# ScalarE's queue between the products, an uneven split of the second matmul, and an interleaved change of layers in a fused attention and two-layer kernel

## The chip, the cores and the metric

The kernel runs on one core of a Trainium2 chip. The metric is the device time of one execution in microseconds (us). The engines are named as in the profile: PE is TensorE (PEld its weight loads), DVE is VectorE, ACT is ScalarE, POOL is GpSimd, SP is SyncE, which here issues the DMAs.

## The reference

```
attn: q, k, v (8 batches, 8 heads, 576 tokens, 64 wide), in chunks of 64 tokens
      softmax(q_c k_c^T / 8) v_c                     -> x, 4608 tokens x 512
layer 1: h = x @ w_in (512 x 2048); g = s * relu(h)**2 + b; y = g @ w_out (2048 x 512)
layer 2: h = y @ w2_in;  P = a0 + a1 h + a2 h^2 + a3 h^3
         Q = 1 + |b0||h| + |b1| h^2;  g = P / (Q + 1e-6);  out = g @ w2_out
```

Everything is float32; the moe weights arrive as 64-bit floats, which the kernel decodes on DVE.

## The kernel before

**Blocks.** The 4608 tokens are 36 tiles of 128 in ten blocks. Blocks 0 and 1 (two tiles each) go through layer 1 in float32, while the weights are loaded and decoded. Blocks 2 to 9 (four tiles each) use fp16 pairs, a high and a low part of each number, and three matmuls for a product of two pairs. Attention of later tiles, decoding of layer 2's weights, and the scaling of finished blocks run beside the matmuls of earlier blocks.

**A group.** The first matmul of layer 1 is done by one level of a Strassen scheme: seven products of 12 matmuls of 256 columns (`product`, L445). `l1_group(j, u, ...)` computes a quarter (u = 0 to 3) of block j's 2048 hidden columns, so there are 32 groups. A group has four quarters. (0) Products 1 and 7 go into two PSUM banks, Z and Y; ACT copies Y to SBUF (L504) and then Z over Y (L505). (1) Products 2 and 6 follow, 2 into Y and 6 into Z; ACT takes Y out with a relu (L512) and copies Z over Y again (L513). (2) Products 4 and 5; DVE adds the earlier copy to each and thereby empties both banks (L518, L519); ACT does relu, square and the fp16 rounding (L521, L491, L492), DVE the low part (L493). (3) Product 3 into Z, and the same for the other half (L526, L491, L492, L493). The next group's Z and Y use the same two banks, so its product 7 needs the bank that L526 empties.

**What fills the gaps.** After each of the four quarters stands a piece of the *second* matmul of the group before: `m2(n)` issues the 12 matmuls of 512 columns of quarter `QO[n]` (L484). So PE has other work while ACT makes the copy that product 2 or product 4 waits for. Four PSUM banks collect y; when a block is complete, ACT takes them out (L547).

**Jobs.** `at(slot, fn, ...)` puts other work into slots, four slots to a group, and `jobs_at(n)` runs those of a slot at the head of a quarter: attention (`at_amx` squares v on ACT, L232, once v is loaded; `at_score` L263; `at_exp` L274 to L276; `at_prob` L287 to L290; `at_pv` L311, whose result goes from PSUM to the block's x by an ACT copy, L315), the splitting of x and y into fp16 pairs by pieces (`x_piece`, `y_piece`: L414 on ACT, L415 on DVE, seven for a block in the order `YORD`), and the decoding of layer 2's weights on DVE (L141 to L144, L586) after a DMA has brought them (L130). There is one x tile for the block being assembled: the next block's first L315 has to wait until all seven pieces of the block before have been read. The score of a tile goes into two PSUM banks, one of which the attention's second product uses as well.

**The order.** Instructions are written in one program order, and a scheduler decides, engine by engine, in which order they are queued, from the dependencies and a model of durations. Each engine then runs its queue in that order. `tc.issue_after(ins)` adds an edge: what is traced under it is queued behind `ins` on the engine of `ins`.

**Layer 2** does the same with the second set of weights and a longer chain on ACT and DVE (`chain_a` to `chain_e`, L946 to L978). Its second matmul lags two groups behind, so its first two groups have none of it between their products. The change of layers: the last group's second matmul (48 matmuls) and the last twelve before it stand in one run, then layer 2's group 0 begins; its copies on ACT are L1049, L1061, L937 and L1071.

Of the kernel before, what the change touches and what calls it, by code (L numbers as in the profile page):

```python
# [20 lines left out]
def attn_moe_moe2(ctx: ExitStack, tc: tile.TileContext, qk, v, w_in, w_out, s_in, b_in,  # L21
# [28 lines left out]
    wo1_p = ctx.enter_context(tc.tile_pool(name="wo1", bufs=KF + 1, reuse_waits="tile"))  # L50
    wi1a_p = ctx.enter_context(tc.tile_pool(name="wi1a", bufs=14, reuse_waits="tile"))
    y1_p = ctx.enter_context(tc.tile_pool(name="y1", bufs=1, reuse_waits="tile"))
    ps_y = ctx.enter_context(tc.tile_pool(name="psy", bufs=1, space=PS))
# [338 lines left out]

    YORD = ("11", "T3", "21", "T1", "22", "T2", "T4")
    t2 = {}
# [77 lines left out]

    gq = {}

    def l1_y2(j, u, q):
        if u + q == 2 and u == 0:
# [4 lines left out]
        for dd in range(KD):  # L481
            for m, (a, l) in enumerate(TERMS):
                o = a * 512 + dd * 128
                T.matmul(out=ybank[j][dd], lhsT=wo1.hl[f][:, o:o + 128], rhs=g[:, l],  # L484
                         start=(first and m == 0), stop=(last and m == 2))
        if q == 1:
            gq.pop((j, u))
# [7 lines left out]
    def l1_group(j, u, jobs_at, m2):  # L495
        x = xhl[j]
        bank = lambda nm: ps_h.tile([128, 2, 256], F32, name=nm, tag="h")
        half = lambda: l1_p.tile([128, 2, 2, 256], F32, name="h1", tag="h1")
        jobs_at(0)
        Z, Y = bank("bZ"), bank("bY")  # L500
        product(wi1, x, u, "1", Z, True)
        product(wi1, x, u, "7", Y, True)
        p7 = l1_p.tile([128, 2, 256], F32, name="sn", tag="sn", bufs=3)
        A.activation(out=p7, in_=Y, func=AF.Copy)  # L504
        A.activation(out=Y, in_=Z, func=AF.Copy)  # L505
        m2(0)
# [4 lines left out]
        g = gq[j, u] = l1_p.tile([128, 2, 2, 1024], F16, name="g", tag="g")  # L511
# [143 lines left out]
    def l2_consts():  # L655
# [19 lines left out]
        V.tensor_tensor(out=dlt, in0=dlt, in1=bt[:, 0:1], op=ALU.mult)  # L675

    start = [KF * j for j in range(NB + 1)]
# [37 lines left out]
    bufs = ((y1_p, "y32"), (raw_p, "raw"), (l1_p, "g"), (l1_p, "g"))  # L715

# [33 lines left out]

    at(start[3], l2_consts)

    if True:
# [75 lines left out]
        g_step()  # L829
        while pend_y:  # L830
            y_step()

        prev = None
        QO = (2, 3, 0, 1)

        def m2_of(u):
            def m2(n):
                if u is None:
                    return
                l1_y2(*u, QO[n])  # L840
                if u[1] == 3 and n == 3:
                    y_later(u[0])
            return m2
# [3 lines left out]

        def l1_slot(slot):
            j, k = slot // KF, slot % KF
            run_jobs(slot)  # L850
            if j == NB - 1:
# [10 lines left out]
        for j in range(NFULL, NB):  # L862
            if j == NB - 1:
                right.close()
                w2_p = ctx.enter_context(tc.tile_pool(name="w2", bufs=14, side="right", reuse_waits="tile"))
                w2_fetch(quads[0])
            for u in range(4):
                l1_group(j, u, lambda n: l1_slot(start[j] + 4 * u + n), m2_of(prev))
                prev = (j, u)
        m2 = m2_of(prev)  # L870
        for n in range(4):
            m2(n)
        while wo2.todo:
            wo2.fetch(wo2.todo.pop(0))
        while wo2.cut:
            wo2.split(wo2.cut.pop(0))
        late = sorted(jobs)
        left.close()
# [3 lines left out]
        yin = {}  # L882
        par = {}
# [8 lines left out]
        def l2_par(j):  # L892
            tn = lambda n, nm: l2_p.tile([128, n], F32, name=nm, tag=nm, bufs=3)
            c = tn(1, "c")
            V.scalar_tensor_tensor(out=c, in0=invy[j], scalar=16.0, in1=wi2.inv, op0=ALU.mult, op1=ALU.mult)
            m = tn(4, "m")
            hb = tn(1, "hb")
            V.tensor_scalar(out=hb, in0=c, scalar1=2.0 ** 26 * float(DM) ** 0.5, scalar2=None, op0=ALU.mult)
            V.memset(m[:, 0:1], 1.0)
            V.tensor_tensor(out=m[:, 1:2], in0=hb, in1=rb[:, 0:1], op=ALU.min)  # L900
            V.tensor_tensor(out=m[:, 2:3], in0=hb, in1=hb, op=ALU.mult)
            V.tensor_tensor(out=m[:, 2:3], in0=m[:, 2:3], in1=rb[:, 1:2], op=ALU.min)
            V.tensor_tensor(out=m[:, 3:4], in0=m[:, 2:3], in1=hb, op=ALU.mult)
            V.tensor_tensor(out=m, in0=m, in1=aabs, op=ALU.mult)
            gm = tn(1, "gm")
            V.tensor_reduce(out=gm, in_=m, axis=AX.X, op=ALU.add)
            V.tensor_scalar(out=gm, in0=gm, scalar1=TINY, scalar2=None, op0=ALU.max)
            e = l2_p.tile([128, 1], I32, name="ge", tag="ge", bufs=3)
            V.tensor_scalar(out=e, in0=gm.bitcast(I32), scalar1=EXPMASK, scalar2=None, op0=ALU.bitwise_and)
            ig = tn(1, "ig")  # L910
            V.tensor_scalar(out=ig, in0=e.bitcast(F32), scalar1=2.0 ** -14, scalar2=None, op0=ALU.mult)
            na = tn(4, "na")
            V.reciprocal(out=na[:, 0:1], in_=ig)
            for i in range(1, 4):
                V.tensor_tensor(out=na[:, i:i + 1], in0=na[:, i - 1:i], in1=c, op=ALU.mult)
            V.tensor_tensor(out=na, in0=na, in1=a2_sb, op=ALU.mult)
            bc = tn(1, "bc")
            V.tensor_tensor(out=bc, in0=gam, in1=c, op=ALU.mult)
            ao = tn(1, "ao")
            V.tensor_tensor(out=ao, in0=ig, in1=wo2.inv, op=ALU.mult)  # L920
            par[j] = (na, bc, ao)

# [41 lines left out]
        def chain_d(i, sl):  # L964
            na, bc, ao = par[seq[i][0]]
            if sl[0] == 0:
                s2[i].append(l2_p.tile([128, 2, BIG], F16, name="g2", tag="g2", bufs=2))
            v, e, r = (t[:, sl[0]:sl[1]] for t in s2[i][:3])
# [32 lines left out]
        l2_load(0)  # L1001
        l2_par(0)
        prime = ps_a.tile([128, 512], F32, name="prime", tag="x")
# [4 lines left out]
        for i in range(N):  # L1008
            for q in range(4):
# [5 lines left out]
                m4[step][slot].append((i, q))  # L1015
        late = [fn for slot in late for fn in jobs.pop(slot)]
        extra = {}
        for n, (fn, args) in enumerate(late):
            if fn is y_piece:
                extra.setdefault(4 + 2 * YORD.index(args[1]), []).append((fn, args))  # L1020
            else:
                extra.setdefault(2, []).append((fn, args))

        def run_m4(i, slot):
            for u in m4[i][slot]:
                l2_y(*u)

        for i in range(N + 2):
            cur, c = i < N, i - 1
            sl = (parts if c in (0, N - 1) else full) if 0 <= c < N else []  # L1030
            if cur:
                j, u = seq[i]
                if u == 1 and j + 1 < NB2:
                    l2_par(j + 1)
# [76 lines left out]
```

## Time and profile before

| | |
|---|---|
| runs | 1607.34, 1609.14, 1614.02 us (median 1609.14) |
| profiled execution | 1607.84 us, of which the profile's span is 1606.0 |
| busy share of the span | PE 96%, DVE 82%, ACT 60% |
| mean granted TensorE clock | 0.988 |
| layer 1 in fp16 | about 160 to 871 us |
| change of layers | about 871 to 907 us |
| layer 2 | about 907 to 1606 us |

A share of busy time is a mean over the whole span; what a stage waits for has to be read from that stage. Times in the trace are counted from the start of the span, and the 1.8 us outside it are in the run's time alone.

### The profile page before, as it was taken

What the parts mean: (1) busy time and instruction counts of PE and PEld (TensorE: products, weight loads), DVE (VectorE), ACT (ScalarE), POOL (GpSimd) and SP (SyncE); (2) the same over time, 40 slices, a digit from 0 to 9 for tenths busy, and PEclk for the clock granted to TensorE, in tenths of its full rate; (3) what the DMA queues carried; (4) which work ended last, traced back from release to release, by engine and by line L of the source; (5) the groups of instructions that cost most, each with busy time, mean ns of one, the idle gap of its engine ahead of it and who ended that gap; (6) DMA issues with size and microseconds to landing.
All of it is one profiled execution on the core that took longest, in us unless ns stands there. A gap on an engine that the chain in (4) does not pass through costs nothing.

```text
span 1606.0 us, 29660 instructions
## 1 busy us (share of the span) xinstructions
PE 1540.4 (96%) x12501; PEld 1042.7 (65%) x12501; DVE 1315.2 (82%) x1980; ACT 966.9 (60%) x1268; POOL 21.9 (1%) x57
## 2 busy tenths in 40 slices
PE   7999999899998999999999899999999999999998
PEld 6878666566665656666665666666666666666664
DVE  7998768778787777665683999999998989888887
ACT  3577856555664655656675756555555565656564
POOL 0000000000000000000000000000000000000000
PEclk8999999999999999999999999999999999999999
DMA  7722214435343353311133020101010101010100
GB/s 278 272 86 62 59 48 163 159 99 171 106 139 128 119 165 96 99 30 57 41 125 115 24 73 27 47 27 47 27 47 27 47 28 47 27 47 28 33 27 27
DMA packets 86118, 131.43 MB, mean 82 GB/s; under 512 B 39648, under 2 KB 39648, under 8 KB 85984
## 3 DMA queue, kind: packets, MB, share of 16 engines
q1 hardware_dynamic: 85984, 129.53, 24.9%
q8 instruction: 98, 1.61, 0.4%
q14 instruction: 36, 0.29, 0.1%
HBM read 86.77 MB, written 34.34 MB: 75 GB/s over the span
## 4 chain that ended last, share of the span: by engine, by line
PE 54%; DVE 26%; ACT 10%; DMA 5%; issue 5%; POOL 0%; SPq 0%; POOLq 0%; ACTq 0%; DVEq 0%
PE y L989 21%; PE bZ L445 13%; PE bY L445 8%; PE y L484 6%; PE bC L445 2%; DVE bits L143 2%; DVE wf L144 2%; ACT h L491 2%; DVE yhl L415 2%; DMA raw<-in_moe_w_in_dram 1%; ACT g L492 1%; DMA raw<-in_moe_w_out_dram 1%; ACT h L521 1%; DVE bits L141 1%; DVE whl L620 1%
## 5 line engine op out<-in xcount | busy, mean ns | idle before, releaser
L445 PEld LDWEIGHTS <-whl 128*128 128x128 f16 x5712 | 560.2, 99 | 164.7 <-issue 50.8
L445 PE MATMUL bZ<-xhl,whl 128*128 128x256 f16 x3264 | 406.2, 275 | 2.8 <-ACT sn L937 1.1
L989 PE MATMUL y<-whl,g 128*128 128x512 f16 x1728 | 396.1, 379 | 3.1 <-DVE g L978 3.1
L484 PE MATMUL y<-g,whl 128*128 128x512 f16 x1536 | 352.3, 379 | 1.0 <-ACT y L547 0.8
L445 PE MATMUL bY<-xhl,whl 128*128 128x256 f16 x2016 | 252.1, 276 | 37.3 <-ACT bY L505 20.2
L989 PEld LDWEIGHTS <-g 128*128 128x128 f16 x1728 | 168.7, 98 | 178.7 <-DVE g L978 4.6
L484 PEld LDWEIGHTS <-whl 128*128 128x128 f16 x1536 | 150.3, 98 | 156.6 <-issue 2.1
L1071 ACT ACTIVATE h<-bZ 128x512 f32<-128x512 f32 x36 | 21.4, 595 | 235.6 <-PE bZ L445 188.4
L493 DVE TENSOR_TENSOR g<-h,g 128x1024 f16<-128x1024 f32 x64 | 78.3, 1223 | 75.9 <-ACT g L492 75.8
L955 DVE SCALAR_TENSOR_TENSOR v<-v,c 128x2048 f32<-128x2048 f32 (+1 forms) x42 | 85.7, 2044 | 37.3 <-ACT v L946 37.3
L956 DVE TENSOR_TENSOR e<-e,h 128x2048 f32<-128x2048 f32 (+1 forms) x42 | 83.0, 1981 | 10.1 <-ACT e L947 10.1
L970 DVE SCALAR_TENSOR_TENSOR g<-e,na,r 128x2048 f16<-128x2048 f32 (+1 forms) x42 | 85.7, 2045 | 5.5 <-ACT r L962 2.4
L957 DVE SCALAR_TENSOR_TENSOR e<-e,na,h 128x2048 f32<-128x2048 f32 (+1 forms) x42 | 85.7, 2045 | 0.8
L977 DVE SCALAR_TENSOR_TENSOR e<-e,na,v 128x2048 f32<-128x2048 f32 (+1 forms) x42 | 85.7, 2044 | 0.8
L971 DVE SCALAR_TENSOR_TENSOR v<-v,g 128x2048 f32<-128x2048 f32 (+1 forms) x42 | 83.2, 1984 | 1.0
L978 DVE TENSOR_TENSOR g<-e,r 128x2048 f16<-128x2048 f32 (+1 forms) x42 | 82.9, 1977 | 0.1
L947 ACT ACTIVATE e<-h,na 128x2048 f32<-128x2048 f32 (+1 forms) x42 | 77.2, 1842 | 6.8 <-DVE g L978 6.8
L946 ACT ACTIVATE v<-h,bc 128x2048 f32<-128x2048 f32 (+1 forms) x42 | 73.6, 1756 | 7.7 <-DVE h L1065 6.5
L961 ACT ACTIVATE r<-v,c 128x2048 f32<-128x2048 f32 (+1 forms) x42 | 73.5, 1755 | 1.0 <-DVE v L955 1.0
L962 ACT ACTIVATE r<-r,c 128x2048 f32<-128x2048 f32 (+1 forms) x42 | 73.3, 1755 | 1.0
L491 ACT ACTIVATE h<-h 128x1024 f32<-128x1024 f32 x64 | 67.5, 1054 | 1.6
L492 ACT ACTIVATE g<-h 128x1024 f16<-128x1024 f32 x64 | 67.5, 1054 | 1.6
(189 smaller groups left out, 1767.8 us busy)
## 6 DMA issues: line engine op xcount, KB each, us to landing
qk<-in_qk_dram SPq DMA_DIRECT2D x36, 512.0 KB, 3.5
raw<-in_moe_w_in_dram SPq DMA_DIRECT2D x16, 1024.0 KB, 5.5
raw<-in_moe_w_out_dram SPq DMA_DIRECT2D x16, 1024.0 KB, 5.8
v<-in_v_dram SPq DMA_DIRECT2D x36, 256.0 KB, 2.7
out_dram<-o SPq DMA_DIRECT2D x36, 256.0 KB, 2.1
yd<-yhl SPq DMA_DIRECT2D x27, 256.0 KB, 2.2
xhl<-yd SPq DMA_DIRECT2D x27, 256.0 KB, 2.6
w2din<-wf SPq DMA_DIRECT2D x16, 256.0 KB, 2.0
```

The costliest lines, as they stand in the source:

```text
L445: T.matmul(out=b[:, s, :], lhsT=t[:, a, o:o + 128], rhs=x[pk][:, l, kk, :], start=start and s + kk + n == 0, stop=stop and s + kk + n == 4 ...
L484: T.matmul(out=ybank[j][dd], lhsT=wo1.hl[f][:, o:o + 128], rhs=g[:, l], start=(first and m == 0), stop=(last and m == 2))
L491: A.activation(out=hf, in_=hf, func=AF.Square)
L492: A.activation(out=g[:, 0], in_=hf, func=AF.Copy)
L955: V.scalar_tensor_tensor(out=v, in0=v, scalar=dlt, in1=v, op0=ALU.add, op1=ALU.mult)
L956: V.tensor_tensor(out=e, in0=e, in1=hh, op=ALU.mult)
L957: V.scalar_tensor_tensor(out=e, in0=e, scalar=na[:, 1:2], in1=hh, op0=ALU.add, op1=ALU.mult)
L970: V.scalar_tensor_tensor(out=g[:, 0], in0=e, scalar=na[:, 0:1], in1=r, op0=ALU.add, op1=ALU.mult)
L971: V.scalar_tensor_tensor(out=v, in0=v, scalar=q0c, in1=g[:, 0], op0=ALU.add, op1=ALU.mult)
L977: V.scalar_tensor_tensor(out=e, in0=e, scalar=na[:, 0:1], in1=v, op0=ALU.add, op1=ALU.subtract)
L978: V.tensor_tensor(out=g[:, 1], in0=e, in1=r, op=ALU.mult)
L989: T.matmul(out=ybank[j][t], lhsT=g[:, a, q, t * 128:(t + 1) * 128], rhs=w[:, l * 512:(l + 1) * 512], start=(u + q == 0 and m == 0), stop=( ...
```

## The change

1. In a group, `jobs_at(n, ins)` passes an ACT instruction, and the slot's jobs are traced under `issue_after` of it: in quarter 0 the last group's relu of product 3, in quarter 1 the first copy of Z over Y, in quarters 2 and 3 the second one.
2. The sixteen parts of the second matmul (four quarters q by four output banks dd, three matmuls each) are dealt to the four gaps as 5, 5, 4, 2 instead of 4, 4, 4, 4. The remaining steps of the float32 second matmul go into the gaps of the first group.
3. `YORD` puts piece 22 last; the x pieces lie in slots 0, 0, 1, 2, 2, 3, 4 counted from the first instead of 0, 0, 1, 1, 2, 2, 3.
4. The last group's second matmul goes between the products of layer 2's group 0. The splits of layer 2's output weights that were left over follow at the ends of its groups 0 and 1, and `l2_par` of blocks 0 and 1 (some twenty DVE instructions on a few columns each) moves into layer 1's last block. The g tiles of both layers share one pool.

```diff
-    YORD = ("11", "T3", "21", "T1", "22", "T2", "T4")
+    YORD = ("11", "T3", "21", "T1", "T2", "T4", "22")
...
-        jobs_at(0)
+        jobs_at(0, crit.get("h"))
...
-        A.activation(out=Y, in_=Z, func=AF.Copy)
+        c = A.activation(out=Y, in_=Z, func=AF.Copy)
         m2(0)
-        jobs_at(1)
+        jobs_at(1, c)
...
-        A.activation(out=Y, in_=Z, func=AF.Copy)
+        c = A.activation(out=Y, in_=Z, func=AF.Copy)
         m2(1)
-        jobs_at(2)
+        jobs_at(2, c)
...
-        jobs_at(3)
+        jobs_at(3, c)
         product(wi1, x, u, "3", Z, False, True)
-        A.activation(out=h0[:, :, 1], in_=Z, func=AF.Relu, scale=16.0 * C1)
+        crit["h"] = A.activation(out=h0[:, :, 1], in_=Z, func=AF.Relu, scale=16.0 * C1)
...
+    XS = (0, 0, 1, 2, 2, 3, 4)
...
-            at(slot + 1 + m // 2, x_piece, j, p)
+            at(slot + 1 + XS[m], x_piece, j, p)
...
-        while pend_y:
-            y_step()
...
-        QO = (2, 3, 0, 1)
+        M2U = [(q, dd) for q in (2, 3, 0, 1) for dd in range(KD)]
+        M2C = (0, 5, 10, 14, 16)
...
                 if u is None:
+                    if pend_y:
+                        y_step()
                     return
-                l1_y2(*u, QO[n])
+                for q, dd in M2U[M2C[n]:M2C[n + 1]]:
+                    l1_y2(*u, q, dd)
...
-            run_jobs(slot)
+            with tc.issue_after(after.ins) if after else ExitStack():
+                run_jobs(slot)
...
-        m2 = m2_of(prev)
-        for n in range(4):
-            m2(n)
...
+        last_m2 = m2_of(prev)
...
+            if i == 0:
+                last_m2(slot)
```

ACT's queue before, in the last group of block 3 (the stretch from about 318 us). `wsq` is the squared v, `xhl` a piece of x, `sn` and `bY<-bZ` the two copies, `h<-bY` the relu, `e` the exponential of the attention:

```order
L232 ACTIVATE wsq,am<-v 128x512
L414 ACTIVATE xhl<-x_3144,c_238 128x512
L414 ACTIVATE xhl<-tx,c_238 128x512
L414 ACTIVATE xhl<-x_3144,c_238 128x512
L504 ACTIVATE sn<-bY 128x512
L414 ACTIVATE xhl<-x_3144,c_238 128x512
L505 ACTIVATE bY<-bZ 128x512
L512 ACTIVATE h_4318<-bY 128x2x256
L414 ACTIVATE xhl<-x_3144,c_238 128x512
L276 ACTIVATE e<-e 128x512
L513 ACTIVATE bY<-bZ 128x512
```

The same group in the changed kernel (lines are one higher, L506 and L514 are the copies of Z over Y):

```order
L505 ACTIVATE sn<-bY 128x512
L506 ACTIVATE bY<-bZ 128x512
L290 ACTIVATE ph<-e 128x512
L415 ACTIVATE xhl<-x_3149,c_241 128x512
L415 ACTIVATE xhl<-tx,c_241 128x512
L513 ACTIVATE h_4324<-bY 128x2x256
L514 ACTIVATE bY<-bZ 128x512
L277 ACTIVATE e<-e 128x512
L415 ACTIVATE xhl<-x_3149,c_241 128x512
L233 ACTIVATE wsq,am<-v 128x512
L415 ACTIVATE xhl<-x_3149,c_241 128x512
```

The square of v, the pieces of x and the exponential have moved from in front of the two copies to behind them.

ACT's queue in the changed kernel behind that group, in the first group of block 4 (`x_3149` is the x of the block before, `x_4400` the next block's, written by L316 from the bank `xp`):

```order
L505 ACTIVATE sn<-bY 128x512
L506 ACTIVATE bY<-bZ 128x512
L290 ACTIVATE ph<-e 128x512
L415 ACTIVATE xhl<-x_3149,c_241 128x512
L316 ACTIVATE x_4400<-xp,xsc 128x4x128
L513 ACTIVATE h_4622<-bY 128x2x256
L514 ACTIVATE bY<-bZ 128x512
```

The last piece of the old x now stands behind this group's copies, and the first L316 of the new x behind that piece; before, the L315 that answers to it stood in the group before, ahead of that group's relu L526.

The same first group of block 4 further on, before, from the relu of products 4 and 5 to that of product 3 (L491 and L492 are square and rounding, `vs` is v scaled for the attention, `y` the output banks):

```order
L521 ACTIVATE h_4617<-h_4617 128x1024
L491 ACTIVATE h_4617<-h_4617 128x1024
L492 ACTIVATE g<-h_4617 128x1024
L315 ACTIVATE x_4395<-xp,xsc 128x4x128
L246 ACTIVATE vs<-v,sc 128x512
L526 ACTIVATE h_4616<-bZ 128x2x256
```

And in the changed kernel:

```order
L522 ACTIVATE h_4623<-h_4623 128x1024
L492 ACTIVATE h_4623<-h_4623 128x1024
L548 ACTIVATE y_4778<-y_3623,c_257,al 128x512
L493 ACTIVATE g<-h_4623 128x1024
L316 ACTIVATE x_4400<-xp,xsc 128x4x128
L548 ACTIVATE y_4778<-y_3624,c_257,al 128x512
L527 ACTIVATE h_4622<-bZ 128x2x256
```

The scaling L246 has gone behind the relu of product 3, and two of the four evictions of y have come ahead of it. This is so in the first groups of seven blocks; in most other groups the scaling alone has left, and in one of four L315 with it.

At the change of layers, in ACT's queue between layer 2's copies L1071 (now L1078) and L1049 (now L1056), two of the four parts of `chain_a` (L946, L947) have moved ahead of the first, and two evictions of layer 1's last y and one more split of an output weight (L184, now L185) have come in.

## Rows read from the trace of the kernel before

**Rows 1.** The page's first part: busy us, share of the span, instructions.

```profile
PE 1540.4 (96%) x12501; PEld 1042.7 (65%) x12501; DVE 1315.2 (82%) x1980; ACT 966.9 (60%) x1268; POOL 21.9 (1%) x57
```

**Rows 2.** Windows: stretch, length, busy us of each engine, clock, DMA.

```profile
160.00:871.00 711.00, 672.19 (x6412) 447.50 (x6410) 517.26 (x1070) 447.35 (x658) 16.16 (x39) 0.99 0.34 107
```

**Rows 3.** PE's waits from 160 to 871 us: total, times, longest.

```profile
PE bY L445 <- ACT bY L505: 20.2, 15, 2.8
PE bY L445 <- ACT bY L513: 14.7, 11, 3.2
PE bY L445 <- ACT h L526: 2.0, 2, 1.2
```

**Rows 4.** Timeline from 280 us: start, length, instruction, idle before and its releaser.

```profile
294.00 0.63 ACT L232 ACTIVATE wsq<-v 128x512 bf16<-128x512 f32 x1 [2.14 <-DMA v<-in_v_dram]
...
295.24 0.58 ACT L505 ACTIVATE bY<-bZ 128x512 f32<-128x512 f32 x1
...
295.88 1.47 PE L445 MATMUL bY<-xhl,whl 128*128 128x256 f16 x12 [1.22 <-ACT bY L505]
...
300.06 0.43 DVE L141 TENSOR_SCALAR bits<-raw 128x512 int32<-128x512 int32 x1 [4.13 <-DMA raw<-in_moe_w_in_dram]
...
303.31 0.63 ACT L276 ACTIVATE e<-e 128x512 f32<-128x512 f32 x1 [5.28 <-DVE e L275]
...
304.48 1.47 PE L445 MATMUL bY<-xhl,whl 128*128 128x256 f16 x12 [3.23 <-ACT bY L513]
...
310.65 1.48 PE L445 MATMUL bZ<-xhl,whl 128*128 128x256 f16 x12
...
313.77 0.71 ACT L246 ACTIVATE vs<-v,sc 128x512 f16<-128x512 f32 x1
...
314.38 0.58 ACT L526 ACTIVATE h<-bZ 128x512 f32<-128x512 f32 x1
...
315.87 1.47 PE L445 MATMUL bY<-xhl,whl 128*128 128x256 f16 x12
...
318.64 0.63 ACT L232 ACTIVATE wsq<-v 128x512 bf16<-128x512 f32 x1 [1.50 <-DMA v<-in_v_dram]
...
322.76 0.58 ACT L505 ACTIVATE bY<-bZ 128x512 f32<-128x512 f32 x1
...
323.39 2.72 PE L445 MATMUL bY<-xhl,whl 128*128 128x256 f16 x12 [2.83 <-ACT bY L505]
```

**Rows 5.** Window behind that last wait; columns as in rows 2.

```profile
323.20:326.70 3.50, 3.31 (x16) 2.31 (x16) 3.47 (x9) 0.64 (x3) 0.00 (x0) 0.51 0.02 8
```

**Rows 6.** Groups by line and shape, 240 to 616 us: count, busy us, mean ns.

```profile
L414 ACT ACTIVATE xhl<-x,c 128x512 f16<-128x512 f32 x20 | 14.2, 712 | 1.8 <-DVE c L391 1.8
...
L415 DVE SCALAR_TENSOR_TENSOR xhl<-x,c,xhl 128x512 f16<-128x512 f32 x19 | 14.2, 746 | 0.1
...
L547 ACT ACTIVATE y<-y,c,al 128x512 f32<-128x512 f32 x16 | 11.4, 769 | 0.0
...
L315 ACT ACTIVATE x<-xp,xsc 128x512 f32<-128x512 f32 x16 | 10.7, 670 | 0.0
...
L289 ACT ACTIVATE ph<-e 128x512 f16<-128x512 f32 x16 | 10.1, 630 | 43.8 <-DVE e L287 43.8
```

**Rows 7.** The chain that ended last: start, time it took, what.

```profile
203.69 2.59 PE y L484 x12
206.28 1.31 PE bY L445 x12
```

**Rows 8.** Timeline of the change of layers; columns as in rows 4.

```profile
891.28 1.47 PE L445 MATMUL bZ<-xhl,whl 128*128 128x256 f16 x12 [1.05 <-ACT sn L937]
...
895.79 0.58 ACT L1071 ACTIVATE h<-bZ 128x512 f32<-128x512 f32 x1
...
902.15 0.58 ACT L1049 ACTIVATE bC<-bZ 128x512 f32<-128x512 f32 x1
...
902.77 0.49 PE L445 MATMUL bC<-xhl,whl 128*128 128x256 f16 x3 [4.12 <-ACT bC L1049]
```

More of the change, by code (lines that the diff above doesn't have):

```diff
@@ L473, in attn_moe_moe2, with l1_y2 @@
     gq = {}
-    def l1_y2(j, u, q):
-        if u + q == 2 and u == 0:
+    crit = {}
+    def l1_y2(j, u, q, dd):
+        if (u, q, dd) == (0, 2, 0):
             ybank[j] = new_y()
@@ L480, in l1_y2 @@
         g = gq[j, u][:, :, q // 2, (q % 2) * 512:(q % 2 + 1) * 512]
[L481 to L486, printed above, removed]
+        for m, (a, l) in enumerate(TERMS):
+            o = a * 512 + dd * 128
+            T.matmul(out=ybank[j][dd], lhsT=wo1.hl[f][:, o:o + 128], rhs=g[:, l],
+                     start=(first and m == 0), stop=(last and m == 2))
+        if (q, dd) == (1, KD - 1):
             gq.pop((j, u))
@@ L675, in l2_consts, with l2_par @@
         V.tensor_tensor(out=dlt, in0=dlt, in1=bt[:, 0:1], op=ALU.mult)
+    par = {}
+    def l2_par(j):
+        tn = lambda n, nm: y1_p.tile([128, n], F32, name=nm, tag="p" + nm, bufs=3 if nm in ("na", "bc", "ao") else 1)
+        c = tn(1, "c")
+        V.scalar_tensor_tensor(out=c, in0=invy[j], scalar=16.0, in1=wi2.inv, op0=ALU.mult, op1=ALU.mult)
+        m = tn(4, "m")
+        hb = tn(1, "hb")
+        V.tensor_scalar(out=hb, in0=c, scalar1=2.0 ** 26 * float(DM) ** 0.5, scalar2=None, op0=ALU.mult)
+        V.memset(m[:, 0:1], 1.0)
+        V.tensor_tensor(out=m[:, 1:2], in0=hb, in1=rb[:, 0:1], op=ALU.min)
+        V.tensor_tensor(out=m[:, 2:3], in0=hb, in1=hb, op=ALU.mult)
+        V.tensor_tensor(out=m[:, 2:3], in0=m[:, 2:3], in1=rb[:, 1:2], op=ALU.min)
+        V.tensor_tensor(out=m[:, 3:4], in0=m[:, 2:3], in1=hb, op=ALU.mult)
+        V.tensor_tensor(out=m, in0=m, in1=aabs, op=ALU.mult)
+        gm = tn(1, "gm")
+        V.tensor_reduce(out=gm, in_=m, axis=AX.X, op=ALU.add)
+        V.tensor_scalar(out=gm, in0=gm, scalar1=TINY, scalar2=None, op0=ALU.max)
+        e = y1_p.tile([128, 1], I32, name="ge", tag="pge", bufs=1)
+        V.tensor_scalar(out=e, in0=gm.bitcast(I32), scalar1=EXPMASK, scalar2=None, op0=ALU.bitwise_and)
+        ig = tn(1, "ig")
+        V.tensor_scalar(out=ig, in0=e.bitcast(F32), scalar1=2.0 ** -14, scalar2=None, op0=ALU.mult)
+        na = tn(4, "na")
+        V.reciprocal(out=na[:, 0:1], in_=ig)
+        for i in range(1, 4):
+            V.tensor_tensor(out=na[:, i:i + 1], in0=na[:, i - 1:i], in1=c, op=ALU.mult)
+        V.tensor_tensor(out=na, in0=na, in1=a2_sb, op=ALU.mult)
+        bc = tn(1, "bc")
+        V.tensor_tensor(out=bc, in0=gam, in1=c, op=ALU.mult)
+        ao = tn(1, "ao")
+        V.tensor_tensor(out=ao, in0=ig, in1=wo2.inv, op=ALU.mult)
+        par[j] = (na, bc, ao)
     start = [KF * j for j in range(NB + 1)]
@@ L751, in attn_moe_moe2 @@
     at(start[3], l2_consts)
+    at(start[NB - 1] + 2, l2_par, 0)
+    at(start[NB - 1] + 3, l2_par, 1)
     if True:
@@ L867, in attn_moe_moe2 @@
             for u in range(4):
-                l1_group(j, u, lambda n: l1_slot(start[j] + 4 * u + n), m2_of(prev))
+                l1_group(j, u, lambda n, c: l1_slot(start[j] + 4 * u + n, c), m2_of(prev))
                 prev = (j, u)
-        m2 = m2_of(prev)
-        for n in range(4):
-            m2(n)
[L873 to L877, printed above, removed]
         left.close()
@@ L890, in l2_load @@
                 yin[j][p] = t
[L892 to L921, printed above, removed]
         seq = [(j, u) for j in range(NB2) for u in range(4)]
@@ L1015, in attn_moe_moe2, with late_jobs @@
                 m4[step][slot].append((i, q))
-        late = [fn for slot in late for fn in jobs.pop(slot)]
         extra = {}
[L1018 to L1022, printed above, removed]
+        def late_jobs():
+            for fn, args in [fn for slot in sorted(jobs) for fn in jobs.pop(slot)]:
+                extra.setdefault(4 + 2 * YORD.index(args[1]) if fn is y_piece else 3, []).append((fn, args))
+            for n in range(len(wo2.cut)):
+                extra.setdefault(n * 2 // len(wo2.cut), []).append((lambda: wo2.split(wo2.cut.pop(0)), ()))
+        last_m2 = m2_of(prev)
         def run_m4(i, slot):
@@ L1026, in run_m4 @@
                 l2_y(*u)
+            if i == 0:
+                last_m2(slot)
+                for _ in range((len(wo2.todo) + 3 - slot) // (4 - slot)):
+                    wo2.fetch(wo2.todo.pop(0))
+                if slot == 3:
+                    late_jobs()
         for i in range(N + 2):
```

13 lines of the change are left out of this document (6 added, 7 removed).

## The prediction

> **What bounds the kernel now.** I read the page's shares first: PE is busy for 96% of the span [rows 1], so what can be won is its idle time and the time that it runs at less than full clock. Then the windows by stage. In the 711 us of layer 1 in fp16, PE is busy for 672.2 [rows 2]; 38.8 us are idle, more than half of the 65.6 of the whole span. Over the same stretch the list of PE's waits has 20.2 us in 15 waits for ACT's copy L505, 14.7 in 11 waits for the copy L513, and 2.0 in two for the relu L526 [rows 3]. Every entry has ACT as the releaser, though ACT is busy for 60% of the span. So it isn't ACT's speed but what stands ahead of the copy in its queue, and the timeline shows it. At 294.00 ACT starts the squaring L232 after 2.14 idle us, released by the DMA that brings v; only behind it run the copies, and product 2 has stood for 1.22 [rows 4]. At 303.31 the exponential L276 starts after 5.28 us of idling; L513 is behind it, and product 4 has waited for 3.23. What the exponential waited for is DVE, which stood for 4.13 us at L141 until a DMA had brought raw weights [rows 4]. At 318.64 it is L232 again, with four pieces of x (L414) behind it, and product 2 waits for 2.83 [rows 4].
>
> **A second cost of those waits.** Behind that wait the 12 matmuls took 2.72 us and not 1.47 [rows 4]. The window of 3.5 us there has a granted clock of 0.51, thus the level of 1.2 GHz [rows 5]; PE had stood just before. The stretches behind the other three waits above 2.2 us that I looked at in this stage are like it, four in all. In 3.5 us at half speed 1.75 us of work is lost, say 1.7 a time.
>
> **Part 1, the order on ACT.** Both copies now lead and the jobs follow. A copy then starts when its product has ended, and it has a piece of the second matmul as cover: 12 such matmuls take 2.59, 12 of a product 1.31 [rows 7], so a part of three is 0.65. The new pieces are 3.24, 3.24, 2.59 and 1.30. Two copies in a row need 2 times 0.58 [rows 4], well under 3.24, so the two entries go: 20.2 + 14.7 = **34.9 gained**. What could be left of them is ACT being held in an earlier job when the copy comes up, and the crowded first groups of the stage, where blocks in float32 still need it; I leave **1.5 lost** for that (0 to 5).
>
> The jobs pay. The square now waits for v behind the copies, where nothing of this group is queued but the next relu. The one job that PE itself waits for soon is the eviction of the attention's second product, L315 (now L316). The score of a tile takes two banks, and one is what L316 empties. In the first group of a block, L316 stands behind the last piece of the old x, and that one behind the new copies. From the end of product 7: the two copies 2 x 0.58 [rows 4], the exponential's fp16 part 0.63, the piece on ACT 0.71, its low part on DVE 0.75, L316 0.67 [rows 6]. That is 3.92, with 0.05 for each of six hand-offs (copy ends 323.34, product starts 323.39 [rows 4]) 4.2, against the cover of five parts, 3.24. So at least about 1.0 is uncovered; where ACT comes late out of the group before, by one L414 and one L493 of about a microsecond, it is 2.7. I take 1.5, nearer the hand sum, for seven blocks: **10.5 lost** (0, if the old x's last piece is ahead in time, to 19).
>
> **Part 2, the uneven split.** The first two covers grow by 0.65, which is worth nothing once the copies are prompt. The last shrinks by 1.30. After product 3 the next product 7 needs the bank that the relu L526 empties, with the last piece and product 1 as cover: 2.59 + 1.31 before, 1.30 + 1.31 = 2.61 now. In the group at 310.65 product 3 starts and so ends at 311.96; the relu ran from 314.38 to 314.96, product 7 started at 315.87 [rows 4]. Product 7 would now be wanted at 314.57. In an ordinary group the scaling L246, which started at 313.77 [rows 4], has gone behind the relu; that then ends at 314.35, just in time. In the first groups of seven blocks two evictions of y, 0.77 each [rows 6] and some 0.67 from start to start, have come ahead of the relu: 314.35 + 1.34 = 315.69, so product 7 waits for 1.1. Seven times is 7.8; with 1.0 for other late groups, **8.8 lost** (2 to 15; the upper bound is what I get by putting the new cover on all 32 relus as they were timed before).
>
> **Part 3, the pieces of x** move by up to a slot; their cost is in the block's start above. The products of the new block that read piece 22 are the last to start, so I count no more.
>
> **The clock.** Four spells times 1.7 is 6.8. Half of it comes back, **3.4 gained** (0 to 6.8), since waits at the starts of blocks can put new ones there.
>
> **Part 4, the change of layers.** PE waits there twice: 1.05 for L937 and 4.12 for L1049 [rows 8]. With the 48 matmuls (16 parts, 10.4 us) between the products of layer 2's group 0, the first wait is covered. For the second, PE has 1.30 + 1.31 and the piece after product 4, 2.59, thus 5.2, as cover. On ACT it was 6.4 from L1071's start to L1049's [rows 8]: 0.6 for the copy and 0.64 for each of nine operations behind it. Now two evictions (0.77 each) and a split come in and four of the nine go, which makes 6.0; the four stand ahead of L1078 instead, 2.6 us, and I let half of that delay it, 7.3 in all. So 2.2 stay: 1.05 + 1.9 = **2.9 gained** (0 to 5.2). `l2_par` on DVE and the late splits lie beside matmuls; uncovered, each of some twenty small DVE instructions would cost a few tenths, some 4 us in all. The shared g pool keeps two buffers for a layer; its reuse is hidden as long as the second matmul of a group ends before the group after next begins.
>
> **The sum.** 34.9 - 1.5 - 10.5 - 8.8 + 3.4 + 2.9 = 20.4. The profiled execution took 1607.84 us, 1606.0 of it the span; 1587.4 is what the sum gives, and the median of the runs is 1.3 above that execution, so I say **1588**.
>
> **The rivals.** *The new waits are hidden* (0.22): the last piece of x is done early because ACT idles less, the evictions fall elsewhere. Then 34.9 + 6.8 + 2.9 - 1.5 - 2 = 41, thus about 1567. For it: ACT has 40% of its time free. Against it: both sums are longer than their covers. *Half eaten* (0.15): the upper bounds, 19 and 15, and no clock back: 34.9 - 1.5 - 19 - 15 + 2.9 = 2.3, thus 1606. *The banks, not the queue* (0.06): product 2 waits because both banks are taken, so a prompt ACT changes nothing but the change of layers, 1605. Against it: product 7 ended at 317.18 and its bank could have been emptied, but L505 started at 322.76, with ACT idle for 1.50 of that at L232 [rows 4]. The Trainium skill ("Perfetto Trace Analysis", section "Optimization Strategy") says that a gap that repeats on the engine that should be saturated can mean too little SBUF or PSUM for the next tile; by it, more banks and not this change would be the remedy, and the time would be this rival's 1605. The trace speaks against it here, by the 1.50 idle microseconds at L232 just named. *The shorter last piece decides* (0.07), the slower one: product 7 waits for L526 in all 32 groups, because slot 3's jobs and DVE's adds come later than before (DVE standing at L141 for 4.13 as at 300.06 [rows 4] would do it). The gains 34.9 + 3.4 + 2.9 = 41.2 are used up at 1.3 a group; at 1.75, 56 are lost and the time is 1623.
>
> **How the numbers follow.** The forecast has 0.50, with 1578 to 1598 as its own range. Half a per cent, 8 us, is about what a measurement here can tell from no change, so faster is below 1601. The forecast, the first rival and a third of the second give 0.77; the rest of the second and the banks 0.16; slower 0.07. The range reaches down to the first rival's 1567 and up to 1604, near the second's.
>
> **What the profile after would show.** The waits of product 2 and 4 for the copies near zero; PE idle for about 25 us from 160 to 871; about seven waits of 1 to 2.7 us of the score (L263, now L264) for L316, one at each block's start, and about seven of product 7 for the relu of near 1.1, a group later; spells of half clock down from four to two; 0 and 2.2 at the change of layers, and layer 2 unchanged. Waits for L316 that are absent, or relu waits in every group, would make the number wrong to one side or the other.

## The result and the profile after

The changed kernel takes 1592.74 us (median of four runs, 1590.89 to 1593.58) against 1608.24 before: ratio 0.9896, 95% interval 0.9869 to 0.9924. That is 15.5 us less; 20 were forecast, with a range from the first rival's 1567 up to 1604. The profiled execution took 1593.58 us, 1591.8 of it the span, 14.2 less than the span before.

The page's first part, to be held against [rows 1]: TensorE's idle time is down from 65.6 to 47.5 us, but its busy time is up by 3.9 with the same 12501 matmuls; the section on the prediction comes back to that.

```profile
PE 1544.3 (97%) x12501; PEld 1046.6 (66%) x12501; DVE 1317.2 (83%) x1980; ACT 962.1 (60%) x1268; POOL 24.1 (2%) x57
```

The windows place it. The stretches are cut at the start of the last relu of product 3 in layer 1 (871.2 us before, 858.3 after); columns as in [rows 2]. First the kernel before, then the changed one.

```profile
172.00:871.20 699.20, 662.90 (x6265) 439.65 (x6264) 506.30 (x1046) 437.08 (x641) 16.16 (x39) 0.99 0.34 107
871.20:1606.00 734.80, 720.55 (x4813) 471.06 (x4811) 658.45 (x569) 423.56 (x407) 0.40 (x1) 1.00 0.12 38
```

```profile
172.00:858.30 686.30, 666.19 (x6296) 442.92 (x6297) 522.57 (x1140) 440.82 (x658) 19.12 (x40) 0.99 0.36 110
858.30:1591.80 733.50, 718.38 (x4807) 469.52 (x4805) 654.35 (x499) 423.62 (x407) 0.74 (x1) 1.00 0.12 37
```

Up to that relu the changed kernel is 12.9 us shorter, behind it 1.3. Two parts of the second matmul, 1.3 us, now stand ahead of that last relu and stood behind it before. So what stands up to the end of layer 1 gained 14.2, and the change of layers with layer 2 nothing.

PE's waits in the changed kernel from 160 to 856 us (total, times, longest); [rows 3] are their counterpart.

```profile
PE sp L264 <- ACT x L316: 8.9, 6, 4.2
PE bZ L446 <- DVE h L520: 7.4, 5, 3.3
PE y L485 <- ACT g L493: 1.8, 1, 1.8
PE bY L446 <- ACT bY L506: 0.6, 1, 0.6
...
PE bY L446 <- ACT h L527: 0.5, 1, 0.5
```

The copies' 34.9 us are down to 0.6. In their place stand the score's wait for the eviction of x, forecast at 10.5, and one that wasn't forecast: product 3 (into `bZ`) waits for DVE's add L520, which empties product 5's bank. It had 0.6 us before. The relu L527, forecast at 8.8, has 0.5.

The timeline of the changed kernel around the end of block 3 shows both (start, length, instruction, idle before in brackets with its releaser).

```profile
328.49 0.74 DVE L416 SCALAR_TENSOR_TENSOR xhl<-x,c,xhl 128x512 f16<-128x512 f32 x1
...
330.06 0.68 DVE L145 SCALAR_TENSOR_TENSOR wf<-raw,bits 128x512 int32<-128x512 int32 x1
330.66 0.68 DVE L519 TENSOR_TENSOR h<-bY,sn 128x512 f32<-128x512 f32 x1
...
331.33 0.67 DVE L288 TENSOR_TENSOR e<-e,rs 128x512 f32<-128x512 f32 x1
331.92 0.68 DVE L520 TENSOR_TENSOR h<-bZ,sn 128x512 f32<-128x512 f32 x1
...
332.66 1.47 PE L446 MATMUL bZ<-xhl,whl 128*128 128x256 f16 x12 [3.30 <-DVE h L520]
...
339.37 0.58 ACT L505 ACTIVATE sn<-bY 128x512 f32<-128x512 f32 x1
...
339.99 0.58 ACT L506 ACTIVATE bY<-bZ 128x512 f32<-128x512 f32 x1
340.48 0.62 ACT L290 ACTIVATE ph<-e 128x512 f16<-128x512 f32 x1
341.00 0.71 ACT L415 ACTIVATE xhl<-x,c 128x512 f16<-128x512 f32 x1
...
341.21 0.67 PE L264 MATMUL sp<-qk 64*64 64x64 f32 x14
...
341.74 0.75 DVE L416 SCALAR_TENSOR_TENSOR xhl<-x,c,xhl 128x512 f16<-128x512 f32 x1
342.53 0.69 ACT L316 ACTIVATE x<-xp,xsc 128x512 f32<-128x512 f32 x1 [0.82 <-DVE xhl L416]
...
343.27 0.68 PE L264 MATMUL sp<-qk 64*64 64x64 f32 x18 [1.39 <-ACT x L316]
```

DVE has no idle time among the rows from 328.49 to 331.92: low parts of x pieces, decoding and softmax run ahead of and between the two adds. From 339.37 on ACT goes through the chain that the prediction added up: two copies, L290, the piece, its low part on DVE, L316. The first copy starts at 339.37 and L316 ends at 343.22, 3.85 us later, against 4.2 in the sum.

### The profile page after: what moved, and what is told of

Its sections match the earlier page's. It is cut to its first block, busy times and chain, and to the rows that moved or that the text cites. A ratio compares the mean times of both kernels' runs of the same rounds, so it can differ in the third digit from the quotient of the medians.

```text
span 1591.8 us, 29579 instructions
## 1 busy us (share of the span) xinstructions
PE 1544.3 (97%) x12501; PEld 1046.6 (66%) x12501; DVE 1317.2 (83%) x1980; ACT 962.1 (60%) x1268; POOL 24.1 (2%) x57
## 4 chain that ended last, share of the span: by engine, by line
PE 62%; DVE 22%; ACT 7%; DMA 4%; issue 4%; POOL 0%; SPq 0%; DVEq 0%; ACTq 0%; POOLq 0%
PE y L989 18%; PE bZ L446 15%; PE y L485 11%; PE bY L446 10%; DMA raw<-in_moe_w_in_dram 2%; PE bC L446 2%; DVE bits L144 2%; PE hp L455 1%; DVE wf L145 1%; PE y L468 1%; DVE e L957 1%; DVE e L977 1%; DVE e L956 1%; DVE v L971 1%; PE sp L264 1%
## 5 line engine op out<-in xcount | busy, mean ns | idle before, releaser
L1078 ACT ACTIVATE h<-bZ 128x512 f32<-128x512 f32 x36 | 21.5, 596 | 224.8 <-PE bZ L446 173.0
L494 DVE TENSOR_TENSOR g<-h,g 128x1024 f16<-128x1024 f32 x64 | 78.2, 1221 | 35.9 <-ACT g L493 35.9
L522 ACT ACTIVATE h<-h 128x1024 f32<-128x1024 f32 x32 | 33.8, 1056 | 115.6 <-DVE h L520 115.6
L970 DVE SCALAR_TENSOR_TENSOR g<-e,na,r 128x2048 f16<-128x2048 f32 (+1 forms) x42 | 85.7, 2044 | 5.3 <-ACT r L962 2.2
L947 ACT ACTIVATE e<-h,na 128x2048 f32<-128x2048 f32 (+1 forms) x42 | 77.3, 1842 | 11.6 <-DVE g L978 11.6
L946 ACT ACTIVATE v<-h,bc 128x2048 f32<-128x2048 f32 (+1 forms) x42 | 73.8, 1759 | 15.0 <-DVE h L1072 13.9
L492 ACT ACTIVATE h<-h 128x1024 f32<-128x1024 f32 x64 | 67.4, 1053 | 1.0
```

The source lines that it names most:

```text
L494: V.tensor_tensor(out=g[:, 1], in0=hf, in1=g[:, 0], op=ALU.subtract)
L947: A.activation(out=e, in_=hh, func=AF.Identity, scale=na[:, 3:4], bias=na[:, 2:3])
L970: V.scalar_tensor_tensor(out=g[:, 0], in0=e, scalar=na[:, 0:1], in1=r, op0=ALU.add, op1=ALU.mult)
```

## The experiments

Each ratio is against the kernel before, timed beside the run. Where ratios are compared, the text says if their 95% intervals overlap. Waits are those of the one profiled execution of each kernel.

**The order on ScalarE alone.** To the kernel before, only `jobs_at(n, ins)` with its edges is added.

```diff
-        jobs_at(1)
+        jobs_at(1, c)
...
-            run_jobs(slot)
+            with tc.issue_after(after.ins) if after else ExitStack():
+                run_jobs(slot)
...
```

> The kernel before with only the jobs queued behind the copies (no uneven split, old order of the x pieces, old change of layers). Theory, the order on ScalarE carries the gain: the waits for the two copies fall from 34.9 us to under 4, product 3 waits for DVE's add for some 5 to 8, the start of a block is no worse than before since the last piece of x is a slot earlier; the change of layers stays at 5.2. Time 1590 to 1597. Rival, the other parts carry it: the copies' waits move to the score or to the adds in full and the time stays at 1604 to 1610.

Measured 1584.72 us, ratio 0.9846 (0.9829 to 0.9864): one of the four parts alone gains 1.54%, some 24 us, more than the whole change; the intervals don't overlap. Its waits from 160 to 862 us:

```profile
PE bZ L445 <- DVE apm L103: 8.1, 4, 3.5
PE bY L445 <- ACT bY L506: 4.3, 6, 1.3
PE bZ L445 <- DVE h L520: 2.7, 4, 1.2
...
PE bY L445 <- ACT bY L514: 1.0, 2, 0.7
PE sp L263 <- ACT x L315: 0.2, 1, 0.2
```

The copies keep 5.3, the score waits for 0.2. The first row is product 3's wait for the adds too: L103 is a 0.14 us operation that started at 327.77, as the add behind which it was queued, L520 at 327.17, came to its end, and product 3 started at 327.90; the trace names what came last.

**The other parts alone.** In the changed kernel the jobs may again stand ahead of the copies.

```diff
-            with tc.issue_after(after.ins) if after else ExitStack():
-                run_jobs(slot)
+            run_jobs(slot)
```

> The changed kernel with the jobs again free to stand ahead of the copies: the uneven split, the late x pieces and the interleaved change of layers alone. Theory: the copies' waits stay above 25 us, since jobs that wait for a DMA or for DVE are still ahead of them, the longer first covers take at most 0.65 off each; time 1600 to 1610. Rival, the longer covers and the later pieces are enough: copies' waits under 12, time under 1595.

Measured 1608.18 us, ratio 1.0012 (0.9998 to 1.0026), as the theory had it in the time, but not in the waits, where it said that the copies would keep over 25 us. They keep 14.0 (the two last rows):

```profile
PE bY L446 <- ACT h L527: 17.1, 22, 2.0
PE bZ L446 <- DVE h L520: 12.7, 14, 2.8
PE bY L446 <- ACT bY L514: 7.2, 10, 1.9
PE bY L446 <- ACT bY L506: 6.8, 14, 0.9
```

So the longer first covers and the later pieces together take 21 us off the copies, and the relu takes 17.1 back, in 22 of the groups, and DVE's adds another 12.7. This is the mechanism of the slower rival; it came true with ACT's old order only. The time stays the same although TensorE's idle time, 72.8 us, is 7.2 above the kernel before's: its busy time is 3.7 lower, and half clock costs 1.7 us in this stage instead of 7.8 (by the sum explained under the clock below).

**The equal split.** `M2C = (0, 4, 8, 12, 16)` in the changed kernel.

```diff
-        M2C = (0, 5, 10, 14, 16)
+        M2C = (0, 4, 8, 12, 16)
```

> The changed kernel with the second matmul dealt 4, 4, 4, 4 again. Theory, the split is worth little once the copies are prompt: the two copies need 1.2 of a cover of 2.6, so they stay near 0.6; the four waits of the score for the eviction of x at a block's start grow by 0.65 each, the waits for the relu (0.5) go. Time 1592 to 1596. Rival A, the shorter last piece costs what the prediction said, 8.8 us: time 1584. Rival B, the longer first covers are what hides the copies: the copies' waits come back by over 8 us, time above 1600.

Measured 1596.21 us, ratio 0.9930 (0.9911 to 0.9947), overlapping with the change's own: the prediction's cost of 8.8 for the split (rival A) is out. The score's waits grow from 8.9 to 11.5 us, which is the theory's four times 0.65 in the total only: at the four places they change by 1.50, 1.02, -0.76 and -0.05, and a fifth goes from 0.16 to 1.09. The copies don't stay at 0.6 as the theory also said; they have 3.3 (2.5 for L506, 0.8 for L514), well under rival B's 8.

**The old x pieces.** In the changed kernel, the order and the slots of the pieces as before.

```diff
-    YORD = ("11", "T3", "21", "T1", "T2", "T4", "22")
+    YORD = ("11", "T3", "21", "T1", "22", "T2", "T4")
-    XS = (0, 0, 1, 2, 2, 3, 4)
+    XS = (0, 0, 1, 1, 2, 2, 3)
```

> The changed kernel with the old order and the old slots of the x pieces. Theory, the late last piece makes the four waits of the score (1.4, 1.4, 1.4, 4.2): these go to under 2 us together, and the waits of product 3 for the add, which stand in the groups into which the pieces crowd, change by less than 3 us. Time 1584 to 1589. Rival, moving the pieces only moves the wait: 1.5 slots earlier they crowd DVE in the group before and product 3's waits grow by the 8 us that the score's lose; time 1591 to 1595.

Measured 1586.53 us, but with runs from 1584.14 to 1592.98; ratio 0.9880 (0.9859 to 0.9901), which overlaps with the change's. Its range spans the theory and the rival. The waits tell more:

```profile
PE bZ L446 <- DVE ape L106: 7.3, 4, 3.2
PE bY L446 <- ACT h L527: 5.7, 7, 1.4
PE bZ L446 <- DVE h L520: 4.1, 4, 1.7
PE bZ L446 <- DVE m L687: 2.0, 1, 2.0
...
PE sp L264 <- ACT x L316: 0.9, 1, 0.9
```

The score's wait goes from 8.9 to 0.9, and as the rival said, the waits come back elsewhere: product 3 now waits 13.4 us instead of 7.4, and the relu 5.7 in seven waits. Three of those stand in first groups of blocks (1.44, 0.70 and 1.45), where the prediction had put them, most others in the last block. TensorE's idle time doesn't fall but rises, from 47.5 to 50.3. That the profiled span is 8.7 shorter all the same is busy time, 11.5 less: the score's line has 5.0 less, and half clock costs 6.3 less (1.5 against 7.7 in this stage). So the theory had the time and the score's waits, but the time wasn't won by fewer waits.

**The parameter chains.** `l2_par` is held on VectorE behind what is written ahead of it.

```diff
+    def l2_par_late(j):
+        with tc.issue_after(last(nc.vector.engine)):
+            l2_par(j)
...
-    at(start[NB - 1] + 2, l2_par, 0)
-    at(start[NB - 1] + 3, l2_par, 1)
+    at(start[NB - 1] + 2, l2_par_late, 0)
+    at(start[NB - 1] + 3, l2_par_late, 1)
...
-                    l2_par(j + 1)
+                    l2_par_late(j + 1)
```

> The changed kernel with the layer-2 parameter chains (l2_par) held on VectorE behind what is written ahead of them, so that three of them no longer stand at 606 to 626 us. Theory: the score's wait of 4.19 at 614 us becomes about 1.4 like the three others, and the time falls by 2.8 to 4.5, to 1588 to 1590. Rival, the chain is hidden and the 4.19 has another cause (the scales of layer 2's weights stand there too): the wait stays above 3 and the time within 1 us of 1592.7.

Measured 1590.91 us, ratio 0.9900 (0.9884 to 0.9915), no difference that can be told. The place in question in the changed kernel, in the timeline:

```profile
609.47 0.15 DVE L701 RECIPROCAL na<-ig 128x1 f32<-128x1 f32 x1
...
609.60 0.69 DVE L607 TENSOR_TENSOR ws<-wq 128x512 f32<-128x512 f32 x1
610.21 1.22 DVE L494 TENSOR_TENSOR g<-h,g 128x1024 f16<-128x1024 f32 x1
611.34 0.69 DVE L608 TENSOR_TENSOR wq<-wq 128x512 f32<-128x512 f32 x1
...
612.61 0.75 DVE L416 SCALAR_TENSOR_TENSOR xhl<-x,c,xhl 128x512 f16<-128x512 f32 x1
613.39 0.69 ACT L316 ACTIVATE x<-xp,xsc 128x512 f32<-128x512 f32 x1 [3.63 <-DVE xhl L416]
...
614.13 1.12 PE L264 MATMUL sp<-qk 64*64 64x64 f32 x18 [4.19 <-ACT x L316]
```

Parts of the chain (L701) run there on DVE, though the program writes them in layer 1's last block and later: the scheduler has taken them forward. With the chain gone this wait is 3.28 and not 1.4. The combining of layer 2's weights (L607, L608) and L494 remain ahead of the low part, so by these two executions the chain made about a third of the excess over 1.4.

**Order and change of layers, early x pieces.** The equal split, the old x pieces and the late parameter chains together in the changed kernel: what is left of the change is the order on ACT and the change of layers.

```diff
-    YORD = ("11", "T3", "21", "T1", "T2", "T4", "22")
+    YORD = ("11", "T3", "21", "T1", "22", "T2", "T4")
...
-    XS = (0, 0, 1, 2, 2, 3, 4)
+    XS = (0, 0, 1, 1, 2, 2, 3)
...
-    at(start[NB - 1] + 2, l2_par, 0)
+    at(start[NB - 1] + 2, l2_par_late, 0)
...
-        M2C = (0, 5, 10, 14, 16)
+        M2C = (0, 4, 8, 12, 16)
...
```

> Jobs behind the copies, and layer 2's group 0 interleaved with the last second matmul, with the parameter chains held late; x pieces and split as before the change. Theory, the terms add: what the order alone gave (1584.7) less some 1.5 to 3 us at the change of layers, where the waits go from 5.2 to about 4 and the half-clock spell goes: 1581 to 1584. Rival, the interleaving gives nothing, because its shorter waits are paid in layer 2's first groups: 1584 to 1586.

Measured 1580.55 us, ratio 0.9837 (0.9812 to 0.9861), faster than the change as it stands without overlap; against the order alone (0.9846) the intervals overlap, so what the change of layers adds isn't shown by the time. Behind the last relu its window is 733.9 us long, with the same work as the 734.8 before.

**The same with the uneven split.**

```diff
-        M2C = (0, 4, 8, 12, 16)
+        M2C = (0, 5, 10, 14, 16)
```

> The same with the uneven split 5, 5, 4, 2. Theory, with x pieces early the last piece of 1.30 leaves product 7 waiting for the relu at the first groups of blocks, 5 to 8 us (the prediction's 8.8), of which 2 to 4 come back by shorter waits for the copies: 2 to 5 us slower than the even split, 1584 to 1588. Rival, what the split costs at the relu it gains at the copies and in waits elsewhere: within 1 us of the even split.

Measured 1582.85 us, ratio 0.9852 (0.9829 to 0.9876); the intervals overlap. The relu's wait, absent from the run with the equal split, is 5.3 us in four; one of the four (1.45) stands in layer 1's middle, the others in its last block. L506 falls from 3.8 to 0.4, and product 3's waits grow from 9.3 to 12.3.

**Jobs behind the add.** In the kernel with the equal split, the jobs of quarter 3 also stand behind L520 on VectorE.

```diff
-        V.tensor_tensor(out=h1[:, :, 1], in0=Z, in1=p7, op=ALU.add)
+        d = V.tensor_tensor(out=h1[:, :, 1], in0=Z, in1=p7, op=ALU.add)
...
-        jobs_at(3, c)
+        jobs_at(3, c, d)
...
```

> As the run with jobs behind the copies and the interleaved change of layers, and the jobs of quarter 3 also queued on VectorE behind the add that empties product 5's bank. Theory, what product 3 waits for is jobs ahead of that add in VectorE's queue, as the copies waited on ScalarE: its waits (near 10 us) fall by half, time 3 to 6 us below the run without, 1576 to 1581. Rival, VectorE has no room there, so the held jobs come too late for the score or the attention's second product, and as much is lost there: no faster or slower.

Measured 1586.53 us, ratio 0.9873 (0.9851 to 0.9894), which overlaps with the run without. Product 3's waits don't fall but grow from 9.3 to 14.1 us. The theory falls: holding the jobs of this quarter back doesn't make the adds earlier.

**Other splits.** In the kernel with the equal split and early pieces: 4, 3, 5, 4 (shown) and 3, 3, 6, 4, and the equal split again, on one chip.

```diff
-        M2C = (0, 4, 8, 12, 16)
+        M2C = (0, 4, 7, 12, 16)
```

> As the run with jobs behind the copies and the interleaved change of layers, with the second matmul dealt 4, 3, 5, 4. Theory, once the copies are prompt the gap that is short is the one ahead of product 3, where DVE's two adds empty the banks (9.3 us of waits in ten): a part more there takes up to 0.65 from each, a part less ahead of product 4 costs the copy L514 little (1.2 needed, 1.95 left): 3 to 5 us less, 1576 to 1579. Rival, DVE is late by its load and not by the distance, so that the wait moves to the next place where DVE's output is needed: within 1.5 us of the same split in equal parts.

> The same with 3, 3, 6, 4. Theory: the waits for the adds nearly vanish (1.3 more cover against waits of up to 2.2), the copies' waits grow (L506 from 3.8 to some 6, as the last block's ACT work stands in the way): 1575 to 1579. Rival, the copies, whose cover of 1.95 includes ACT's jobs that are still running, come back by more than 6 us: 1581 or above.

> The run with jobs behind the copies and the interleaved change of layers once more, on the same chip as the other two splits: 1578 to 1582, so that the splits are compared on one chip.

Measured 1581.23 (ratio 0.9834, 0.9820 to 0.9849), 1580.68 (0.9825, 0.9809 to 0.9841) and 1583.03 us (0.9850, 0.9827 to 0.9873). The three overlap, and the 3 to 5 us that the theories expected aren't to be seen. The waits move as both sides said; with 3, 3, 6, 4:

```profile
PE bY L446 <- ACT bY L506: 6.7, 9, 1.8
PE bY L446 <- ACT bY L514: 4.9, 6, 2.4
...
PE bZ L446 <- DVE h L520: 2.3, 3, 1.3
```

Product 3's waits, 12.8 us in this chip's equal split, are down to 2.3, the copies' up from 3.6 to 11.6. Cover taken from one gap shows in another.

**Decoding later.** In the kernel with the equal split the decoding of layer 2's weights starts three quarters of a group later.

```diff
-    WS, WP = 24, 4
+    WS, WP = 27, 4
```

> As the run with jobs behind the copies and the interleaved change of layers, equal split, and the decoding of layer 2's weights on VectorE placed three quarters of a group later. Theory, product 3 waits at the ends of four blocks because the decode and the low parts of the x pieces stand together ahead of the adds: with the decode begun behind the adds these waits (5.4 to 9.7 us in two profiles) fall by more than half, and PE's other waits stay; time 1576 to 1580. Rival, the scheduler spreads the decode over the group whatever its slot, and DVE is as late: product 3's waits stay within 3 us, time within 3 us of 1580 to 1583.

Measured 1590.12 us, ratio 0.9875 (0.9852 to 0.9897), which overlaps with both runs without this edit and is no gain. Its waits of product 3:

```profile
PE bZ L446 <- DVE h L520: 12.0, 13, 3.8
```

The four at the ends of blocks, which have a row of their own, stay at 5.9 us (5.4 and 9.7 in the two profiles of the equal split), and the row shown has six of 0.5 to 3.8 us between 302 and 576 us, where the first profile of the equal split has one (0.85). Where the decoding stands matters, since it changes these waits, but this was the wrong way to move it; which DVE work the adds stand behind, and how to order it, stays open.

## Why the prediction came out as it did

**The copies** (34.9 gained, less 1.5 for the first groups): right. 0.6 is left; in the first groups of the stage two other waits of 0.45 and 1.82 remain. The run of the order alone shows that this term carries the whole gain, although 5.3 of the copies' waits stay there; the run without it shows that the other parts gain nothing by themselves. The rival of the missing banks is out: the same two banks serve once the copies are prompt. The Trainium skill ("Perfetto Trace Analysis", section "Optimization Strategy") names too little SBUF or PSUM as something that repeated gaps can mean. It was no more than a possibility here: the gaps went with an order.

**The start of a block** (10.5 lost at seven places): the mechanism was right, the count too high, and a good third of the price was missed. Three waits are of 1.38 to 1.39 us, beside a hand sum of 1.0 and a chosen 1.5. There are four such places and not seven; at the fourth the wait is 4.19, some 0.9 of it from the parameter chains, which the prediction had put beside the matmuls. With two of 0.35 or less the sum is 8.9. But the score that is held runs in two parts: 14 of its 32 matmuls take 0.67 at 341.21, the other 18 take 0.68 at 343.27, where a score that isn't held takes 0.69 for all 32 (366.17). That is counted as busy time, and no list of waits shows it; its size stands under the sum below.

**The shorter last piece** (8.8 lost): the term failed. The sum was made from the group at 310.65 [rows 4], in which DVE's adds came late; in the first groups of blocks they don't. In the first group of block 4 of the changed kernel:

```profile
354.04 2.75 PE L485 MATMUL y<-g,whl 128*128 128x512 f16 x12
...
354.96 1.06 ACT L522 ACTIVATE h<-h 128x1024 f32<-128x1024 f32 x1 [4.80 <-DVE h L520]
...
357.60 1.48 PE L446 MATMUL bZ<-xhl,whl 128*128 128x256 f16 x12
...
359.85 0.60 ACT L527 ACTIVATE h<-bZ 128x512 f32<-128x512 f32 x1
```

From L522 to the relu it is 4.89 us, with the evictions in and the scaling out; in the sum's group it was 4.32 (L521 at 310.06, the relu at 314.38 [rows 4]), so the chain was priced rightly. But product 3 starts 2.6 us after L522 here and 0.6 after L521 there, so the relu ends at 360.45 and product 7, at 361.52, doesn't wait. The 1.39 us for which PE had stood at 343.27, in the same group, are part of the room that ACT and DVE had. Where that wait is gone, with the old x pieces, the relu's wait is there, 5.7 and with late chains 5.3 us, but only some of it in first groups of blocks.

**What took its place**: product 3's wait for the adds, 7.4 us. The prediction knew that DVE can stand at L141, but only as something that delays the relu, with a chance of 0.07 and no price in the sum. It also read that every entry of the list of waits had ACT as the releaser; the last of the five entries was this wait, 0.6 us in two. Product 3 waits for DVE in every version with prompt copies and four parts in its gap: 7.4 us here, 10.8 with the order alone, 13.4 with the old pieces, 9.3 with these and the equal split. That before, PE stood at the copies first, so that DVE had the time to come up, is a reading and not shown: with the other parts alone the copies keep 14.0, and product 3 waits 12.7 all the same. So the two new waits, of x and of the adds, come to 16.3 us against 20.8 forecast for three terms, and the sum of waits looked better than its parts.

**The clock** (3.4 gained): not in layer 1. Between 172 us and that last relu, busy time times what is missing to full clock, added up over windows of 7 us, was 7.8 us before and 7.7 after: five spells of half clock in each, one of them behind the 128 one-column matmuls of `l1_bias`. Ahead of 172 us the same sum rose from 5.6 to 7.2, and behind the last relu it fell from 1.0 to 0.1. The premise was misread: of the six waits above 2.2 us that this stage had before, three stand ahead of half clock (323.39, 445.63 and 606.07) and three don't (164.58, 304.48 and 416.65). Behind 304.48, the longest with 3.23 us, the 12 matmuls took 1.47 [rows 4], and the window there has the full clock:

```profile
304.40:307.90 3.50, 3.42 (x28) 2.74 (x28) 3.04 (x7) 0.45 (x2) 0.00 (x0) 1.00 0.22 80
```

The sum within layer 1 is 5.5 with the order alone, 3.4 with the order, the change of layers and early pieces, and 0.0 with 3, 3, 6, 4. Between the profile of the order alone (span 1584.4) and that with the change of layers (1577.3) 5.8 of the 7.1 us are TensorE's busy time, 2.1 of it clock by this sum, and 1.3 idle time.

**The change of layers** (2.9 gained): nothing in the changed kernel. The waits of 4.12 and 1.05 [rows 8] are 1.92 and 1.26 now. The 1.92 is near the forecast 2.2, but the wait for L937, which was to vanish, is a little longer, and 0.69 for L970 comes in. With the equal split the stretch is shorter than before, by 0.7 to 0.9 in four profiles and by 2.2 in one.

**The sum**: 20.4 forecast, 14.3 between the two profiled executions. The range held because terms erred on both sides. By their waits, relu and start of a block were 11.9 too dear (the relu's old 2.0 went to 0.5, which is 1.5 gained beside 8.8 forecast as lost); the adds, 6.8 more than before, weren't foreseen; the clock, the change of layers and the first groups were some 7 too good. That leaves about 18, which is what TensorE's idle time fell by. The other 3.9 are the busy time that rose, and by line most of the rise is the score's, before and after (count, busy us, mean ns, idle before; lines overlap where one group runs into the next, so they don't add up exactly to the page's busy time):

```profile
L263 PE MATMUL sp<-qk 64*64 64x64 f32 x1152 | 29.0, 229 | 3.5 <-ACT x L315 3.4
L264 PE MATMUL sp<-qk 64*64 64x64 f32 x1152 | 35.3, 233 | 12.1 <-ACT x L316 11.8
```

It is 6.3 us more, 5.8 of them in layer 1 from 160 us on. With these 5.8 and the waits of 8.9 the late x pieces cost some 15 us, against 10.5 forecast. The score needs 34.9 and 33.9 us in the two other runs that have both the new order and the late pieces, but 28.8 with the late pieces and the old order, and 30.4, 30.3 and 30.1 in the first three runs with the new order and early pieces. Against the order alone the profiled span of the changed kernel is 7.4 longer: 4.9 is the difference in the score's line and 2.1 that in idle time. So by these two profiles most of what the bundle lost of its first part's gain is the held scores. That this is the late pieces' doing is told by these lines; by the time it isn't, since the interval of the run with the old pieces overlaps with the change's. That the errors cancelled far enough to leave the total in the range was luck.

## What to carry to other kernels

A bundle of four edits gained 15.5 us where one of them gains some 24: measure each part alone before keeping it. When a wait goes away, another engine can be the next to be late; price the wait for each engine whose output the next steps need, from a group in which that engine is as loaded as it will be. Compare busy time by line as well as waits: a group of matmuls that is held in its middle can cost busy time that no list of waits has. Between gaps of fixed total cover, moving cover moves the wait; the times of the splits that were tried with early pieces can't be told apart.

## What the runs showed of the hardware that was not expected

The half-clock spell doesn't follow the longest wait. One case of the kernel before stands above, under the clock. Windows of 3.5 us in the changed kernel behind four waits, of 3.30, 1.39, 1.38 and 1.39 us; the clock is the number before the last two:

```profile
332.60:336.10 3.50, 3.44 (x26) 2.52 (x26) 3.19 (x7) 3.40 (x4) 0.00 (x0) 1.00 0.08 29
...
343.20:346.70 3.50, 3.43 (x34) 2.62 (x35) 3.18 (x9) 0.61 (x2) 0.00 (x0) 0.69 0.88 213
433.20:436.70 3.50, 3.43 (x43) 3.01 (x44) 3.17 (x9) 0.61 (x2) 0.00 (x0) 1.00 0.78 217
521.20:524.70 3.50, 3.44 (x32) 2.61 (x33) 3.45 (x9) 0.15 (x2) 0.00 (x0) 0.62 0.82 217
```

Behind 3.30 us the clock is full (2.4 GHz), behind two of the three short waits it falls to 1.2 GHz for part of the window. The granted clock also differs between executions of one kernel: in the run of order and change of layers, six executions go from 1574.54 us at a mean of 0.996 to 1584.34 us at 0.989.
